# Linear attention feeding a swish MLP: the load of k of batch 5 issued one block sooner

## The chip, the cores and the metric

The kernel runs on one core of a Trainium2 chip. The metric is device time in microseconds (us) of one execution; the figure for a kernel is the median of its runs. The core has five engines that run beside each other and wait for each other through semaphores: TensorE (PE, matrix products), VectorE (DVE), ScalarE (ACT, activation functions), GpSimd (POOL) and SyncE (SP, which here only starts transfers). Transfers run on 16 DMA engines, fed from queues that an engine's instructions fill.

## The reference

Eight batches of 8 heads, 576 positions and head size 64. First a linear attention with phi(x) = elu(x) + 1, then a two-layer MLP with a swish of learned slope.

```
q_p, k_p = phi(q), phi(k)                 # phi(x) = where(x > 0, x, exp(x) - 1) + 1
kv  = einsum('bhsd,bhse->bhde', k_p, v)
z   = sum(k_p, axis=2)
num = einsum('bhsd,bhde->bhse', q_p, kv)
den = einsum('bhsd,bhd->bhs', q_p, z)[..., None] + 1e-06
x   = (num / den).transpose(0, 2, 1, 3).reshape(4608, 512)
h   = x @ w_in                            # 512 -> 2048
g   = h * (1.0 / (1.0 + exp(-beta * h)))
out = g @ w_out                           # 2048 -> 512
```

## The kernel before, in words

Work is cut by batch. The 576 positions of a batch become four tiles of 128 and a rest of 64; the rests of all eight batches are gathered in `xT_tail` and make a ninth block. A block b of the MLP has an `h_phase` (16 groups of four matmuls, each 128 x 512, into one bank of the four-bank pool `mmps`, each followed by a silu on ACT, lines 454 and 462) and a `y_phase` (four output tiles of 16 matmuls, line 472, evacuated by DVE at line 245 and stored). Batch 0 has a prologue of its own; the loop at line 842 runs the blocks 1 to 8.

The attention of later batches is threaded into these phases as side work. `at(sh, n, ...)` puts a call behind group n of the h phase, `at(sy, n, ...)` behind step n of the y phase (16 steps of four matmuls). In block b, with n = b + 1 and m = b + 2:

- the y phase computes phi of q of batch m (`phi_all(m, "q")`, step 3), starts its transposes by DMA (`q_trans_dma(m)`, tile `qTd`, step 5), and loads q of batch m + 1 (`load_q`, step 5) held by `hold` until the last of these transposes has landed;
- for b below 3, phi of k of batch m is computed there too (step 8);
- from b = 2 on, the two exps of k of batch m + 1 are put at step 10 (`phi_exps`), and the DVE part of phi comes at group 2 of the next h phase (`phi_rest`);
- x of batch n is transposed by DMA from SP (`x_trans_dma`, tiles `xT` and `xT_tail`), and v of batch m + 1 is loaded from SP (step 9).

The order on each engine is the order in which the program emits the calls (a manual schedule). ACT therefore runs the silus of block b + 1 behind the exps emitted in block b. Between exp and silu ACT loads a function table (1.28 us).

Loads of q and k go out from POOL's queue and convert to bf16 on the way. k lives in three buffers `xk`, batch b in `xk[b % 3]`, q likewise in `xq`, so k of batch 5 takes the buffer of batch 2. The exp results `e` have four buffers, two for each phi. Names that the trace shows: `xk<-in_k_dram` is a load of k (line 83), `e<-xk` an exp of k (line 144), `r<-xk` the DVE part (line 148), `g<-h_ps` a silu (line 462).

Before the change k of batch 4 is loaded in block 1, and in block 2 k of batch 5 and k of batch 6 are loaded one behind the other, both behind the held q of batch 5. From block 3 on k is loaded two batches ahead of the phi of q in the same block.

Of the kernel before, what the change touches and what calls it, by code (L numbers as in the profile page):

```python
# [16 lines left out]
def kernel(  # L17
# [62 lines left out]
    def load(eng, dst, src, b, h0=0, n=4):  # L80

        rows = src[b].rearrange("h (g j) d -> (h g) (j d)", j=J)
        return eng.dma_start(  # L83
            out=dst[:, h0 : h0 + n].rearrange("p h j d -> p h (j d)"),
            in_=rows.rearrange("(i p) e -> p i e", p=P)[:, h0 : h0 + n],
        )
# [140 lines left out]
    def num_tile(name):  # L227
        return numps.tile([P, 2, 512], F32, tag="num", name=name)
# [4 lines left out]
    def kv_both(b):  # L233

        t = num_tile("kvp")
        for pr in range(2):
            kv_pair(b, pr, [t[:, hh, pr * EA : (pr + 1) * EA] for hh in range(2)])
        st[b, "kvd"] = work.tile([P, 2, 2 * EA], BF16, tag="kv_bd", name="kvd")
        nc.vector.tensor_copy(st[b, "kvd"], t[:, :, 0 : 2 * EA])
# [32 lines left out]
    def q_trans_dma(b):  # L272
        st[b, "qTd"] = work.tile([P, 4 * J, G], BF16, tag="qT", name="qTd")
        for hh in range(2):
            st[b, "qTd", "dma"] = nc.sync.dma_start_transpose(
                out=st[b, "qTd"][:, hh * 2 * J : (hh + 1) * 2 * J],
                in_=st[b, "q"][hh * G : (hh + 1) * G].rearrange("p a j c -> p (a j c)"),
            )

    def q_odd_trans(b, tp):  # L280

        tv = tp.rearrange("p (a n) -> p a n", a=2)
        for pr in range(2):
            nc.tensor.matmul(
                tv[:, pr], st[b, "q"][:, pr, J - 1, :], identity,
                is_transpose=True, start=True, stop=True, skip_group_check=True,
            )
        nc.scalar.copy(
            q_odd[b].rearrange("p (i a) g -> p a i g", i=2),
            tv.rearrange("p a (i g) -> p a i g", i=2),  # L290
        )
# [30 lines left out]
    def numers(b, after=None):  # L322

        pairs = [num_tile("nps") for _ in range(2)]
        odd = [mm_tile("nps_m") for _ in range(2)]
        if after is not None:
            for pr in range(2):
                kv_pair(after, pr, [pairs[pr][:, hh, 6 * EA : 7 * EA] for hh in range(2)])
        for k in range(2):
            dst = [pairs[k][:, h] for h in range(2)]  # L330
            numer_tile(b, dst, k)
            numer_tile(b, dst, 2, (k,), 4)
        numer_tile(b, odd, 3)
        for hh in range(2):
            quads(b, odd, 4 + hh, lambda c: (c, J - 1), hh, None)
        st[b, "nps"] = pairs, odd
        for k in range(3):
            norms(b, k)
        if after is not None:
            st[after, "kvd"] = work.tile([P, 2, 2 * EA], BF16, tag="kv_bd", name="kvd")  # L340
            for pr in range(2):
                nc.vector.tensor_copy(
                    st[after, "kvd"][:, :, pr * EA : (pr + 1) * EA],
                    pairs[pr][:, :, 6 * EA : 7 * EA],
                )
# [93 lines left out]
    def x_trans_dma(b, t):  # L439
        xv = st[b, "xs", t].rearrange("p n d -> p (n d)")  # L440
        if t < NT - 1:
            nc.sync.dma_start_transpose(out=x_dst(b, t), in_=xv)
            return

        for pr in range(2):
            nc.sync.dma_start_transpose(  # L446
                out=xT_tail[:, places(b, pr), b * G : (b + 1) * G],
                in_=xv[pr * G : (pr + 1) * G, 0 : 2 * P],
            )
# [39 lines left out]
    def load_q(b, after):  # L489
        if b < B:  # L490
            hold(load(nc.gpsimd, xq[b % NX], q, b), after)

    def load_k(b):
        if b < B:
            load(nc.gpsimd, xk[b % NX], k, b)

    def load_v(b):
        if b < B:
            load(nc.sync, vf[b % 2], v, b)

    def phi_exps(b, a):
        for pr in range(2):
            phi_part(b, a, pr, xin(b, a, pr))

    def phi_rest(b, a):
        phi_tile(b, a)
        for pr in range(2):
            phi_relu(b, a, pr, xin(b, a, pr))
        for pr in range(2):
            phi_min(b, a, pr)  # L510

    def phi_all(b, a):
        phi_exps(b, a)
        phi_rest(b, a)

    def v_copies(b):
        for pr in range(2):
            v_copy(nc.gpsimd, b, pr)
# [288 lines left out]
    def h_phase(b, x, side):  # L807
        for ff in range(FC):

            if b == 1 and ff in (3, 4):  # L810
                hp = num_tile("h_ps2")[:, 0]
            else:
                hp = mm_tile("h_ps")
            h_mm(b, x, ff, hp)
            silu(b, ff, hp)
            run(side, ff)

    def y_phase(b, side, last=False):
        for t in range(4):
            if last and t == 3:  # L820
                for c0, c1 in ((0, 320), (320, 512)):
                    yp = mm_tile("y_ps")
                    for i in range(4):
                        y_mm(b, t, i, yp, c0, c1)
                    y_out(b, t, yp, c0, c1, (nc.sync, nc.scalar))
                break
            yp = mm_tile("y_ps")
            halves = ((0, 256), (256, 512)) if b == 1 and t > 1 else ((0, 512),)
            for cols in halves:
                for i in range(4):  # L830
                    y_mm(b, t, i, yp, *cols)
                    if i < 3 and cols is halves[-1]:
                        run(side, 4 * t + i)
            y_out(b, t, yp)
            run(side, 4 * t + 3)

    def at(side, n, *fs):
        side.setdefault(n, []).extend(fs)
# [3 lines left out]
    for b in range(1, B + 1):  # L842
        n = b + 1
        m = n + 1
        sh, sy = {}, {}
        if b == 1:
            at(sh, 0, lambda: q_trans_dma(2))
            at(sh, 1, lambda: v_copies(2))
            at(sh, 2, lambda: load_q(3, st[2, "qTd", "dma"]), lambda: load_k(3))
            at(sh, 2, lambda: load_v(3))  # L850
            at(sh, 7, lambda: q_odd_trans(1, num_tile("qop")[:, 0].bitcast(BF16)[:, 0:256]))
            at(sh, 8, lambda: kv_both(2))
            at(sy, 1, lambda: numers(2))
        elif n < B:
            if b == 2:
                at(sh, 8, odd_numers, odd_norms, lambda: kv_both(3))
                at(sh, 9, lambda: [x_trans_dma(i, 4) for i in range(2)])
            if b == 3:
                at(sh, 8, lambda: kv_both(4))
            if 4 < m < B:  # L860
                at(sh, 2, lambda: phi_rest(m, "k"))
                at(sh, 6, lambda: v_copies(m))
            at(sh, FC - 1, lambda: numers(n, m if 4 < m < B else None))
        if n < B:
            for t in range(NT):
                at(sy, t // 3 + (2 if b == 1 else 0), lambda t=t: x_trans_dma(n, t))
        if m < B:
            at(sy, 3, lambda: phi_all(m, "q"))
            at(sy, 5, lambda: q_trans_dma(m), lambda: load_q(m + 1, st[m, "qTd", "dma"]))
            if b < 3:  # L870
                at(sy, 5, lambda: load_k(m + 1))
                at(sy, 4, lambda: v_copies(m))
                at(sy, 8, lambda: phi_all(m, "k"))
            if b > 1:
                at(sy, 5, lambda: load_k(m + 2))
            at(sy, 9, lambda: load_v(m + 1))
            if 4 < m + 1 < B:
                at(sy, 10, lambda: phi_exps(m + 1, "k"))
        h_phase(b, xT[b % 3] if b < B else xT_tail, sh)
        y_phase(b, sy, last=(b == B))  # L880
# [30 lines left out]
```

## Time and profile before

| | |
|---|---|
| median of 3 runs | 303.47 us (302.96 to 306.81) |
| span of the profiled run | 302.5 us |
| PE busy | 277.7 us, 92% |
| ACT busy | 160.3 us, 53% |
| DVE busy | 108.0 us, 36% |
| POOL busy | 36.8 us, 12% |
| loads of k, full batches | 7 of 576 KB each, median 13.8 us from issue to landing |
| loads of q | 7 of 576 KB each, median 9.6 us |
| mean granted TensorE clock | 0.972 |

Busy time of an engine is the sum of its instructions' spans. Where a view gives a duration and, in brackets, a time with an arrow, the bracket is how long the engine was idle just before and what released it. A wait that the trace puts down to one engine may have had several semaphores; the one that came last is named. The row of slices shows the span in 40 equal parts, each digit the busy share in tenths; the row of the clock shows in the same way what share of full speed the array was granted.

### The profile page before, as it was taken

Reading aid. Unit: us, or ns where it says so; the run is one execution under the profiler, and the core shown is the slowest. Engines: PE = TensorE matmul, PEld = TensorE weight load, DVE = VectorE, ACT = ScalarE, POOL = GpSimd, SP = SyncE. Lnnn points to the kernel's source line nnn. Section 1 sums busy time; section 2 is a strip of 40 time slices with the busy share of each in tenths; the row PEclk is TensorE's granted clock in tenths of the full one; section 3 lists DMA queues with packets and bytes.
Section 4 is the critical chain, followed back from the end, with each engine's and each line's share of the span. In section 5 each row is a group of like instructions: output and inputs, shape, how many; then the busy total and the mean of one; then the engine's idle time right before and its main releaser. Section 6 shows DMA issues by size and latency. Waiting matters only on the chain.

```text
span 302.5 us, 5979 instructions
## 1 busy us (share of the span) xinstructions
PE 277.7 (92%) x2482; PEld 139.7 (46%) x2512; DVE 108.0 (36%) x259; ACT 160.3 (53%) x219; POOL 36.8 (12%) x51
## 2 busy tenths in 40 slices
PE   7899999999999960199999999999999999999995
PEld 2674466447544420045444544454444444444443
DVE  5824489439114810301931274046106100120012
ACT  5888569939467300658718852791372057108600
POOL 8622002140040022000003100300000000000000
PEclk9999999999999996579999999999999999999999
DMA  8999999499499389700379737913801430131022
GB/s 220 206 246 361 275 211 233 85 262 165 111 273 156 78 198 274 121 2 2 74 132 266 139 77 161 280 34 64 200 15 38 107 77 0 35 69 37 0 68 72
DMA packets 51723, 41.03 MB, mean 136 GB/s; under 512 B 31584, under 2 KB 43120, under 8 KB 51696
## 3 DMA queue, kind: packets, MB, share of 16 engines
q1 hardware_dynamic: 38800, 23.61, 32.7%
q0 software_dynamic: 12736, 16.91, 28.7%
q8 instruction: 19, 0.31, 0.4%
q10 hardware_dynamic: 160, 0.13, 0.2%
q14 instruction: 8, 0.07, 0.1%
HBM read 36.71 MB, written 9.44 MB: 153 GB/s over the span
## 4 chain that ended last, share of the span: by engine, by line
PE 81%; DMA 9%; DVE 4%; ACT 2%; SPq 2%; issue 2%; POOL 0%; DVEq 0%; POOLq 0%; ACTq 0%
PE h_ps L454 38%; PE y_ps L472 37%; DMA xk<-in_k_dram 4%; DMA xT_tail<-xs 3%; SPq L446 1%; DMA qTd<-phi_q 1%; DMA stage<-in_q_dram 1%; ACT e L144 1%; PE h_ps L665 1%; PE nps L184 1%; DVE phi_q L155 1%; PE kvp L184 1%; DVE r L148 1%; PE nps L309 1%; DVE y_sb L245 1%
## 5 line engine op out<-in xcount | busy, mean ns | idle before, releaser
L462 ACT ACTIVATE g<-h_ps,beta_c 128x512 bf16<-128x512 f32 x144 | 97.5, 689 | 84.8 <-PE h_ps L454 84.3
L472 PE MATMUL y_ps<-w_out,g 128*128 128x512 bf16 (+4 forms) x621 | 126.5, 359 | 0.9 <-issue 0.2
L454 PE MATMUL h_ps<-xT,w_in 128*128 128x512 bf16 x486 | 111.3, 385 | 17.4 <-ACT g L462 16.8
L454 PEld LDWEIGHTS <-w_in 128*128 128x128 bf16 x560 | 55.0, 99 | 83.7 <-issue 20.6
L472 PEld LDWEIGHTS <-g 128*128 128x128 bf16 x636 | 60.9, 98 | 61.1 <-DVE xs_odd L383 0.3
L245 DVE COPY y_sb<-y_ps 128x512 f32<-128x512 f32 (+2 forms) x37 | 24.9, 672 | 77.4 <-PE y_ps L472 77.4
L144 ACT ACTIVATE e<-xk 128x1152 bf16<-128x1152 bf16 x16 | 17.8, 1154 | 23.8 <-DMA xk<-in_k_dram 23.7
L392 DVE TENSOR_SCALAR den<-nps 128x12 f32<-128x12 f32 x12 | 2.0, 165 | 57.4 <-PE nps L309 57.4
L83 POOL DMA_DIRECT2D xq<-in_q_dram x7 | 5.2, 745 | 107.6 <-DMA qTd<-phi_q 89.5
L144 ACT ACTIVATE e<-xq 128x1152 bf16<-128x1152 bf16 x14 | 15.6, 1155 | 0.8 <-DMA xq<-in_q_dram 0.8
L454 PE MATMUL h_ps<-xT_tail,w_in 128*128 128x512 bf16 x62 | 13.9, 379 | 0.1
L155 DVE TENSOR_TENSOR phi_q<-e,r 128x1152 bf16<-128x1152 bf16 (+2 forms) x17 | 12.5, 765 | 2.7 <-ACT e L144 2.4
L173 POOL CAST vaug<-vf 128x1152 bf16<-128x1152 f32 x10 | 11.2, 1151 | 17.9 <-DMA vf<-in_v_dram 13.3
L383 DVE TENSOR_TENSOR xs<-nps,rden 128x512 bf16<-128x512 f32 (+1 forms) x24 | 12.3, 552 | 1.0 <-DMA xT_tail<-xs 0.4
L144 ACT ACT_TABLE_LOAD x6 | 7.7, 1283 | 8.5 <-DMA xq<-in_q_dram 8.4
L148 DVE TENSOR_SCALAR r<-xk 128x1152 bf16<-128x1152 bf16 x16 | 6.7, 457 | 15.2 <-DMA xk<-in_k_dram 15.2
L155 DVE TENSOR_TENSOR phi_k<-e,r 128x1152 bf16<-128x1152 bf16 x16 | 11.6, 750 | 0.6 <-ACT e L144 0.6
L133 PE MATMUL warm_ps<-xT 128*128 128x512 bf16 x20 | 7.5, 532 | 1.8 <-DVE xT L96 1.5
L462 ACT ACT_TABLE_LOAD x6 | 7.7, 1283 | 0.1
L83 POOL DMA_DIRECT2D xk<-in_k_dram x9 | 6.8, 753 | 4.5 <-DMA g<-in_moe_w_out_dram 2.0
L148 DVE TENSOR_SCALAR r<-xq 128x1152 bf16<-128x1152 bf16 x14 | 6.8, 517 | 1.0 <-DMA xq<-in_q_dram 1.0
L730 DVE TENSOR_SCALAR w_out<-g,rbeta 128x512 bf16<-128x512 f32 x8 | 3.8, 536 | 9.0 <-DMA g<-in_moe_w_out_dram 9.0
(98 smaller groups left out, 117.8 us busy)
## 6 DMA issues: line engine op xcount, KB each, us to landing
out_dram<-y_sb SPq DMA_DIRECT2D x70, 128.0 KB, 2.5
vf<-in_v_dram SPq DMA_DIRECT2D x5, 1152.0 KB, 6.6
xq<-in_q_dram POOLq DMA_DIRECT2D x7, 576.0 KB, 9.6
xk<-in_k_dram POOLq DMA_DIRECT2D x7, 576.0 KB, 13.8
w_in<-in_moe_w_in_dram POOLq DMA_DIRECT2D x4, 512.0 KB, 12.8
g<-in_moe_w_out_dram POOLq DMA_DIRECT2D x2, 1024.0 KB, 17.7
stage<-in_moe_w_out_dram POOLq DMA_DIRECT2D x2, 1024.0 KB, 20.8
stage<-in_q_dram SPq DMA_DIRECT2D x2, 576.0 KB, 4.0
```

What stands on the lines that cost most here:

```text
L83: return eng.dma_start(out=dst[:, h0 : h0 + n].rearrange("p h j d -> p h (j d)"), in_=rows.rearrange("(i p) e -> p i e", p=P)[:, h0 : h0 + n],
L133: nc.tensor.matmul(warm_ps[:, 0:cols], warm[:, 0:P], warm[:, 0:cols], start=True, stop=True)
L144: nc.scalar.activation(st[b, a, pr, "e"][:, :, j0:j1], x[:, :, j0:j1], ACTF.Exp)
L148: nc.vector.tensor_scalar(r, x, 0.0, 1.0, ALU.max, ALU.add)
L155: nc.vector.tensor_tensor(st[b, a][:, pr, j0:j1].rearrange("p j (h d) -> p j h d", h=2), st[b, a, pr, "e"][:, :, j0:j1].rearrange("p h j d ...
L173: eng.tensor_copy(vaug[b % 2][:, pr, :, :, 0:D], src[:, places(b, pr)].rearrange("p h j d -> p j h d"))
L184: nc.tensor.matmul(dst[hh][c], st[b, "k"][r, pr, j, c], mov(r, j, h), start=(j == 0), stop=(j == J - 1), skip_group_check=True,)
L245: eng.tensor_copy(dst, src)
L383: nc.vector.tensor_mul(out, num, rd[..., None].to_broadcast(list(num.shape)))
L454: nc.tensor.matmul(hp[:, c0:c1], w_in_sb[ff // 4][:, kc, (ff % 4) * P : (ff % 4 + 1) * P], x[:, kc, c0:c1], start=(kc == 0), stop=(kc == K ...
L462: nc.scalar.activation(g_sb[b % 2][:, ff, :], hp, ACTF.Silu, scale=beta_c[:, ff : ff + 1])
L472: nc.tensor.matmul(yp[:, c0:c1], g_sb[b % 2][:, ff, t * P : (t + 1) * P], w_out_sb[i][:, c, c0:c1], start=(ff == 0), stop=(ff == FC - 1), ...
```

## The change

The load of k of batch 5 is moved from block 2 to block 1. In block 1, `load_k(4)` is now followed by `load_k(5)` at the same step of the y phase; in block 2, behind the held q of batch 5, only `load_k(6)` is left. Later blocks keep their loads. It is meant to have k of batch 5 in its buffer without waiting for q of batch 5, which is held by the transposes of batch 4.

```
             at(sy, 5, lambda: q_trans_dma(m), lambda: load_q(m + 1, st[m, "qTd", "dma"]))
             if b < 3:
-                at(sy, 5, lambda: load_k(m + 1))
                 at(sy, 4, lambda: v_copies(m))
                 at(sy, 8, lambda: phi_all(m, "k"))
-            if b > 1:
-                at(sy, 5, lambda: load_k(m + 2))
+            if b == 1:
+                at(sy, 5, lambda: load_k(m + 1))
+            at(sy, 5, lambda: load_k(m + 2))
             at(sy, 9, lambda: load_v(m + 1))
```

## The prediction

> **What bounds the kernel now.** I started with the slices of the page. Each slice is 302.5 / 40 = 7.56 us.
>
> ```profile
> PE   7899999999999960199999999999999999999995
> ACT  5888569939467300658718852791372057108600
> PEclk9999999999999996579999999999999999999999
> ```
>
> TensorE (PE) is busy in nine tenths or more of nearly every slice, so it sets the time. There is one hole, in slices 14 to 16 counted from 0 (106 to 128 us), with ScalarE (ACT) empty just before the end of it, and the granted clock falls to 6, 5 and 7 tenths in and after it. The groups then say who waited for whom.
>
> ```profile
> L462 ACT ACTIVATE g<-h_ps,beta_c 128x512 bf16<-128x512 f32 x144 | 97.5, 689 | 84.8 <-PE h_ps L454 84.3
> L454 PE MATMUL h_ps<-xT,w_in 128*128 128x512 bf16 x486 | 111.3, 385 | 17.4 <-ACT g L462 16.8
> L144 ACT ACTIVATE e<-xk 128x1152 bf16<-128x1152 bf16 x16 | 17.8, 1154 | 23.8 <-DMA xk<-in_k_dram 23.7
> ```
>
> The first line is ACT waiting for PE, harmless. The second is the reverse: the h matmuls of line 454 waited 16.8 us for a silu. The third gives the reason: the exps of k waited 23.7 us for a load of k. The chain of waits, taken for 104 to 130 us, puts them in order (start, length, what):
>
> ```profile
> 106.72 3.76 DMA qTd<-phi_q
> ...
> 111.04 0.46 POOL xq L83
> ...
> 111.78 11.65 DMA xk<-in_k_dram
> ...
> 123.51 2.22 ACT e L144 x2
> 125.75 1.28 ACT L462
> 127.04 0.69 ACT g L462
> ```
>
> So at b = 2 the transpose of phi(q) of batch 4 lands, GpSimd (POOL) may then issue q of batch 5 and behind it k of batch 5, that k lands at 123.4, ACT does its two exps and a table load, and only then the first silu of block 3. The timeline of ACT shows which batch each exp belongs to, since it follows program order:
>
> ```profile
> 99.04 2.22 ACT L144 ACTIVATE e<-xk 128x1152 bf16<-128x1152 bf16 x2 [0.63 <-DMA xk<-in_k_dram]
> 123.51 2.22 ACT L144 ACTIVATE e<-xk 128x1152 bf16<-128x1152 bf16 x2 [22.26 <-DMA xk<-in_k_dram]
> ```
>
> The first pair is k of batch 4 (step 8 of y_phase(2)), the second k of batch 5 (step 10). PE had started block 3 at 107.39, filled the four banks of mmps with 16 matmuls by 111.01, and stood until 127.78.
>
> **What the Trainium skill says.** "TensorE: Matmul & The Clock Gate", Part 1, says that an idle array falls to half clock and regains it after about 3.4 us of work. The trace agrees in kind: clock 0.50 in 127.78 to 131.00, 0.75 in 131.00 to 134.77, 1.00 after. The same page (on the architectural detail of the array) says ACT's queue is strict FIFO; the trace agrees, silus whose matmuls had ended by 111 ran at 127.04. "DMA: Bandwidth & Descriptors", section on queues, rings and completion order, says that each DMA engine takes one ring in order and alternates between rings by packets. The trace fits: q and k of batch 4 were issued on GpSimd's queue 0.73 us apart and landed at 94.8 and 99.0, one after the other, while transposes on SyncE's queue beside them took 5 to 9 us instead of 2.4.
>
> **The change, part by part.**
>
> Removed: k of batch 5 from the queue at 111.8, behind q of batch 5. Added: the same 576 KB load at b = 1, right behind q and k of batch 4. Those were issued at 83.63 and 84.36, so k of batch 5 goes out at about 85.1. Nothing holds it there: xk has three buffers and batch 5 takes that of batch 2, whose last reader was done by about 50 us. POOL gets 0.75 us more of issue work at 85.1; it is then idle until 89.09 waiting for v, so that costs nothing. At b = 2 it gets 0.75 us less. No instruction is added or dropped in sum.
>
> When does it land? Behind k of batch 4, which landed at 84.36 + 14.6 = 98.98. Steps from a q to the k behind it, from issue times and landings: 3.6 us (67.9 to 71.5), 4.1 (94.8 to 99.0), 2.8 (120.6 to 123.4), 3.0 (169.2 to 172.2). So 101.6 to 103.1; I take 102.5. ACT is done with the exps of batch 4 at 101.26, and the next e buffer is free after the two phi_q of batch 4 at 102.57 and 103.25. The exps end at about 104.7, the table load of 1.28 us at 106.0. The first h group of block 3 ends near 108.25, so ACT is ready 2 us before it is wanted. PE would only stand if the first silu ended after 111.01, which by 2.22 + 1.28 + 0.73 means a landing after 106.8: 3.7 us of slack against the latest of the four steps.
>
> What it gives is the length of block 3 set against its neighbours, from the list of the chain's pieces and the windows:
>
> ```profile
> 107.39:111.01 3.62, 3.62 (x17) 1.55 (x16) 0.69 (x1) 0.00 (x0) 0.00 (x0) 1.00 0.80 192
> 111.01:127.78 16.77, 0.00 (x1) 0.00 (x0) 2.35 (x4) 4.24 (x5) 4.47 (x5) 0.64 0.97 209
> 127.78:131.00 3.22, 3.22 (x8) 1.17 (x8) 0.00 (x0) 2.37 (x4) 0.00 (x0) 0.50 0.00 0
> 131.00:134.77 3.77, 3.77 (x21) 1.39 (x23) 0.00 (x0) 2.06 (x3) 0.00 (x0) 0.75 0.00 0
> ```
>
> (Columns: window, length, then busy of PE, weight load, DVE, ACT, POOL, then clock.) Block 3 ran from 107.39 to 156.96, 49.57 us. Block 4, 156.96 to 186.02, took 29.06. Block 3 does the same plus one group of 72 small kv matmuls at its step 8 (0.73). So undisturbed it takes 29.8, and **the gain is 49.57 - 29.8 = 19.75**. Made up from its parts: the stand 16.77, and the cold restart, where 20 matmuls took 6.99 us against 20 x 0.216 = 4.32 at the rate of block 4 (37 in 7.99), so 2.67; together 19.44. The two agree within 0.3. I take 19.7.
>
> What is moved costs: packets of k of batch 5 now run from 99 to about 103 beside SyncE's transposes. The one that matters is the last xT of batch 3, issued 100.21, landed 102.5, wanted by PE at 107.39. Bounds: nothing, or 5.1 us as xT took at 94.4 (lands 105.3, no cost), or 9.3 as the slowest xT_tail (lands 109.5, 2.1 us). I take nothing. The transposes of phi(q) of batch 4 go out at 105.33, after it. The y stores hold nobody.
>
> Does a later wait take its place? With block 3 whole, PE wants things 19.7 us sooner. v of batch 5 is issued at 109.78 as before and copied by 118.8; its kv products would be wanted at 141.6 - 19.7 = 121.9: 3.1 us of slack, and less traffic beside it. q of batch 5 (landed 120.6) would be wanted by ACT at 124.0. k of batch 6 moves up into the place of k of batch 5 (123.4) and is wanted at 126.1; even late, ACT has no silu due there until block 4. Blocks 4 and later run as before, shifted: in block 4 k of batch 7 came 172.2 for 174.9 and nobody waited.
>
> Sum: 303.47 - 19.7 = **283.8 us**.
>
> **Rivals.**
>
> A, a part of the hole stays because k of batch 5 lands late. For it: the queues are full from 83 to 99 (summed DMA share 1.2). Against: 3.7 us of slack, and share 0.36 in 99 to 103, where it will run. A landing at 109 gives 2.2 us of stand: 286.0.
>
> B, its packets delay transposes or q and k of batch 4. For it: xT_tail transposes took up to 9.3 us there. Against: in-order rings leave everything before 99 as it was. Gives the 2.1 us above: 285.9.
>
> C, the early load is hidden behind a wait that was there anyway, and nothing is won. It would need something else to keep ACT until 123.5, and its waits name nothing but loads of q and k. 303.
>
> D, slower: the transposes pile up. If each of the four xT of batch 3 took 8.4 instead of 2.4, one after the other, the last lands at 102.5 + 24 = 126.5; PE stands 19.1 us and restarts cold for 2.7: 303.5 - 19.7 + 21.8 = 305.6, more if the qTd transposes then hold q. Against: one load of 576 KB adds about 4 us of traffic.
>
> **How the numbers follow.** Forecast 0.86, A 0.04, B 0.06, C 0.02, D 0.02. The range takes in A and B and half a microsecond of spread below with a somewhat better packed block 3: 282.6 to 286.5. Faster by over 2% (under 297.4): 0.96. Within 2%: C and most of D, 0.03. Slower: 0.01.
>
> **What would show it right or wrong.** Right: an xk load third in POOL's row near 85.1 and only one behind q near 111.8; the wait of the exps for xk of some 23.7 us down to under 3; the 16.8 us of h_ps behind the silu gone; PE's slices all 9 after the first and no dip of the clock; block 3 of about 29.8 us; everything later shifted by the same amount. Wrong at step one if k of batch 5 lands after 106.8; wrong at the transposes if PE starts block 3 later than 107.4; wrong at the later waits if a new stand appears near 122 (v of batch 5) or if blocks 4 to 7 take other than about 29 us.

## The result and the profile after

The changed kernel takes **285.25 us** (median of 4 runs, 285.16 to 285.57) against 303.38 us before (4 runs, 302.96 to 306.81). The ratio is 0.939 with a 95% interval of 0.9327 to 0.9453: 18.1 us less. The profiled execution has a span of 283.5 us. One run of a later experiment (e10: 291.72 us, mean granted clock 0.988 against 1.00 in its other runs, no trace) lies more than 1.5% above the fastest of its kernel and is left out of e10's median and ratio.

The slices of the page after, to be read against those of before:

```profile
PE   7899999999999999999999999999999999999994
PEclk9999999999999999999999999999999999999999
```

The hole in slices 14 to 16 is gone, and so is the dip of the clock behind it. PE is busy for 97% of the span (92% before). In the groups of the page the two waits that carried the argument have shrunk:

```profile
L454 PE MATMUL h_ps<-xT,w_in 128*128 128x512 bf16 x486 | 108.6, 379 | 0.6
...
L144 ACT ACTIVATE e<-xk 128x1152 bf16<-128x1152 bf16 x16 | 17.8, 1151 | 2.5 <-DVE y_sb L245 1.6
```

The h matmuls waited 17.4 us, now 0.6; the exps of k waited 23.8 us, now 2.5. The timeline of POOL after (start, length, what, idle before it) shows the move itself:

```profile
83.87 0.75 POOL L83 DMA_DIRECT2D xq<-in_q_dram  x1 [15.30 <-ACT g L462]
84.61 1.49 POOL L83 DMA_DIRECT2D xk<-in_k_dram  x2
...
110.75 0.75 POOL L83 DMA_DIRECT2D xq<-in_q_dram  x1 [19.09 <-ACT g L462]
111.49 0.76 POOL L83 DMA_DIRECT2D xk<-in_k_dram  x1
```

Two loads of k now follow q of batch 4, and only one is left behind q of batch 5. In the timeline of ACT the exps of batch 5 come 3.8 us after those of batch 4, no longer 24.5:

```profile
98.20 2.20 ACT L144 ACTIVATE e<-xk 128x1152 bf16<-128x1152 bf16 x2
102.04 2.22 ACT L144 ACTIVATE e<-xk 128x1152 bf16<-128x1152 bf16 x2 [1.64 <-DVE y_sb L245]
104.28 1.28 ACT L462 ACT_TABLE_LOAD   x1
```

One caution for the reader. The 1.64 us are put down to a copy of DVE, whose result these exps don't read. The load landed at 102.0: the two loads of k issued from 84.61 on took 13.4 us and, from their median of 15.0, 16.6 us. So that landing released the exps; the copy only ended at the same moment. In a second profile of the changed kernel (e5, below) the same wait is put down to the load:

```profile
100.62 2.22 ACT L144 ACTIVATE e<-xk 128x1152 bf16<-128x1152 bf16 x2 [1.04 <-DMA xk<-in_k_dram]
```

The length of block 3, from its first h matmul to that of block 4, is read in the windows. First before (block 3, block 4), then after (columns: window, length, busy of PE, weight load, DVE, ACT, POOL, clock, share of the DMA engines, GB/s):

```profile
107.39:156.79 49.40, 32.47 (x342) 14.98 (x344) 12.09 (x30) 21.06 (x25) 4.47 (x5) 0.83 0.53 109
156.79:185.86 29.07, 28.91 (x271) 13.73 (x272) 11.39 (x29) 17.89 (x22) 3.73 (x4) 1.00 0.70 161
```

```profile
107.82:137.77 29.95, 29.79 (x342) 14.39 (x344) 11.82 (x30) 17.88 (x22) 3.74 (x4) 1.00 0.73 156
137.77:166.84 29.07, 28.91 (x270) 13.72 (x272) 11.40 (x29) 17.88 (x22) 3.73 (x4) 1.00 0.70 162
```

Block 3 became 19.45 us shorter with the same 342 matmuls, and block 4 has the same length to the hundredth. Block 3 itself starts 0.43 us later (107.82 for 107.39). So the whole gain lies in block 3. That leaves a question: the profiles show 19.45 us, the medians 18.1.

### The profile page after: what moved, and what is told of

Read it like the earlier page. It is cut to its first block, busy times and chain, and to the rows that moved or that the text cites. A ratio compares the mean times of both kernels' runs of the same rounds, so it can differ in the third digit from the quotient of the medians.

```text
span 283.5 us, 5980 instructions
## 1 busy us (share of the span) xinstructions
PE 275.2 (97%) x2482; PEld 139.3 (49%) x2512; DVE 107.9 (38%) x259; ACT 160.5 (57%) x219; POOL 37.8 (13%) x51
## 4 chain that ended last, share of the span: by engine, by line
PE 94%; DMA 2%; DVE 1%; issue 1%; ACT 1%; POOLq 0%
PE y_ps L472 44%; PE h_ps L454 43%; DMA xk<-in_k_dram 2%; PE h_ps L665 1%; PE nps L184 1%; PE nps L309 1%; PE kvp L184 1%; DVE phi_k L155 1%; PE nps_m L309 0%; ACT e L144 0%; PE nps L631 0%; PE tp L655 0%; PE nps L563 0%; PE nps L265 0%; PE dps L546 0%
## 5 line engine op out<-in xcount | busy, mean ns | idle before, releaser
L454 PE MATMUL h_ps<-xT,w_in 128*128 128x512 bf16 x486 | 108.6, 379 | 0.6
L454 PEld LDWEIGHTS <-w_in 128*128 128x128 bf16 x560 | 54.4, 98 | 64.8 <-DVE xT L437 0.3
L184 PEld LDWEIGHTS <-phi_k 64*64 64x64 bf16 x576 | 5.6, 106 | 3.1 <-issue 2.1
## 6 DMA issues: line engine op xcount, KB each, us to landing
xk<-in_k_dram POOLq DMA_DIRECT2D x7, 576.0 KB, 13.4
w_in<-in_moe_w_in_dram POOLq DMA_DIRECT2D x4, 512.0 KB, 12.2
```

The source lines that it names most:

```text
L184: nc.tensor.matmul(dst[hh][c], st[b, "k"][r, pr, j, c], mov(r, j, h), start=(j == 0), stop=(j == J - 1), skip_group_check=True,)
L454: nc.tensor.matmul(hp[:, c0:c1], w_in_sb[ff // 4][:, kc, (ff % 4) * P : (ff % 4 + 1) * P], x[:, kc, c0:c1], start=(kc == 0), stop=(kc == K ...
```

## The experiments

Two things were open: where the missing 1.3 us are, and which wait comes next. "Stand" is PE's wait inside or ahead of block 3. The first theory (K) is that of the prediction: only the landing of k of batch 5 counts, against a limit set by ACT's queue. The rival is B of the prediction: the packets of an early load delay the transposes of x, and PE starts block 3 late.

**How constant is the hole? (e1, e12)** The kernel before, unchanged, profiled twice more.

> The kernel before once more, for its profile. Open is why the gain in the medians (18.1 us) is smaller than the 19.45 us by which block 3 became shorter in the profiles. Theory: the profiled execution of before (304.28 us) was one with a long wait; here the total is near 303.4 and the stand of PE in block 3 is shorter than 16.77 us, by up to 0.9. Rival: the stand is the same within 0.1 and the start of the kernel (up to block 3) differs by some tenths of a us from run to run.

> The kernel before a third time, for its profile: the stand of PE in block 3 was 16.77 us and then 15.69, with 6.99 and 6.31 us for the 20 matmuls behind it. Theory: its total follows these two terms, between 302 and 304.3 us. Rival: another part of the kernel varies as much.

PE's timeline in block 3, of the second execution and then of the third:

```profile
126.50 6.31 PE L454 MATMUL h_ps<-xT,w_in 128*128 128x512 bf16 x20 [15.69 <-ACT g L462]
```

```profile
127.38 6.80 PE L454 MATMUL h_ps<-xT,w_in 128*128 128x512 bf16 x20 [16.37 <-ACT g L462]
```

| execution of before | time | stand | 20 matmuls after it | block 3 |
|---|---|---|---|---|
| first | 304.28 us | 16.77 | 6.99 | 49.40 |
| second | 302.33 us | 15.69 | 6.31 | 47.64 |
| third | 303.69 us | 16.37 | 6.80 | 48.82 |

Stand and restart of the second execution are 1.76 us below the first, of the third 0.59; the times are 1.95 and 0.59 below. So in these three executions nearly all of the scatter comes out of the hole, and the execution I took for the prediction was a long one. The rivals fall: no other part varied as much, and the start of block 3 moved by 0.19 us at most (107.20 for 107.39). My size for e1 was too small, though: the stand fell by 1.08 us, not by up to 0.9, and the total came 1.1 us below the 303.4 I had expected.

**What is the slow restart? (e2)** Matmuls that nobody reads are put where PE stands, in the kernel before.

```
             h_mm(b, x, ff, hp)
+            if b == 3 and ff == 3:
+                fill = num_tile("fill")[:, 0]
+                for _ in range(72):
+                    nc.tensor.matmul(
+                        fill, w_in_sb[0][:, 0, 0:P], w_in_sb[0][:, 0, :], start=True, stop=True
+                    )
             silu(b, ff, hp)
```

> The kernel before with 72 matmuls more in block 3, put on PE where it stands waiting (72 x 0.216 = 15.6 us of the 16.77). Their result is read by nobody. Theory: the wait for k of batch 5 stays as it is, but the array stays warm, so the 20 matmuls behind it take 4.3 us and not 6.99: 2.7 us less than before, 300.7 us, clock 1.00 all through. Rival: the slow restart has another cause (the silus that come in a burst, PSUM banks): no gain, 303.4 us.

301.34 us (5 runs), ratio to before 0.9929 (0.9903 to 0.9956), so 1.3 to 2.9 us less. PE's timeline:

```profile
111.20 15.70 PE L818 MATMUL fill<-w_in 128*128 128x512 bf16 x72
127.39 4.48 PE L454 MATMUL h_ps<-xT,w_in 128*128 128x512 bf16 x20 [0.49 <-ACT g L462]
```

The wait for the load is as long as ever (the exps of batch 5 start at 123.12), yet the same 20 matmuls take 4.48 us, and the granted clock is 1.00 all through the run. The clock is what made them slow; its part is 6.70 - 4.48 = 2.2 us over the mean of the three executions above, not the 2.67 that I took from the first with a full-clock time of 4.32.

**A whole block sooner, or only out of the line? (e3)** k of batch 5 stays in block 2 and is put ahead of the held q.

```
             at(sy, 3, lambda: phi_all(m, "q"))
+            if b == 2:
+                at(sy, 5, lambda: load_k(m + 1))
             at(sy, 5, lambda: q_trans_dma(m), lambda: load_q(m + 1, st[m, "qTd", "dma"]))
+            if b == 1:
+                at(sy, 5, lambda: load_k(m + 1))
             if b < 3:
-                at(sy, 5, lambda: load_k(m + 1))
```

> k of batch 5 stays in block 2 but is issued ahead of the held q of batch 5. Theory (only the place behind the held q counts): POOL comes to it right after its copies of v, at about 91.5 us, it lands near 102, 285.3 us, as with the change. Rival (it must go out a whole block sooner, since the queues of block 2 are full): it lands after 107 and PE stands for some us, 288 to 295 us.

285.37 us (4 runs, ratio 0.9412, 0.9379 to 0.9446). POOL issued it at 90.37, it took 10.0 us, and the exps ran at 101.00; the last thing they waited for was now a buffer that DVE read from. ACT's timeline, then PE's:

```profile
101.00 2.22 ACT L144 ACTIVATE e<-xk 128x1152 bf16<-128x1152 bf16 x2 [1.42 <-DVE phi_q L155]
107.72 7.93 PE L454 MATMUL h_ps<-xT,w_in 128*128 128x512 bf16 x36
```

The 36 matmuls run without a stand, and the time is that of the changed kernel: what counted was the place behind the hold, not the block.

**Without the hold (e4)** The order of before, but q of batch 5 isn't held.

```
-            hold(load(nc.gpsimd, xq[b % NX], q, b), after)
+            d = load(nc.gpsimd, xq[b % NX], q, b)
+            hold(d, after) if b != 5 else None
```

> Order of the loads as before, but q of batch 5 is no longer held by the transposes of phi(q) of batch 4; q of batch 5, k of batch 5 and k of batch 6 all go out at about 91.5 to 93 us. Theory: k of batch 5 is third in line behind k of batch 4, lands near 105, below the limit of about 107: 285.3 us, at most 286. Rival (the hold protects the transposes of batch 3 and 4, which share the DMA engines): the last xT of batch 3 or the qTd of batch 4 land late and PE stands at the start or the end of block 3: 287 us or more.

287.13 us (4 runs, 0.9457, 0.9422 to 0.9492): the rival's number. k of batch 5 landed where I had expected it, and it wasn't what PE waited for. ACT's timeline, then PE's, of this run:

```profile
105.05 2.22 ACT L144 ACTIVATE e<-xk 128x1152 bf16<-128x1152 bf16 x2 [4.96 <-DMA xk<-in_k_dram]
```

```profile
109.78 7.93 PE L454 MATMUL h_ps<-xT,w_in 128*128 128x512 bf16 x36 [2.13 <-DMA xT<-xs]
```

Block 3 began 2.13 us late, because the last transpose of x of batch 3, issued at 99.27, took 10.4 us. The hold that made k of batch 5 late also protects these transposes, so my theory was incomplete.

**How much room is left? (e5 to e8)** The changed kernel again, and with one, two and three loads in front of k of batch 5, into memory that nobody reads (`pad`, three parts of `stage`).

```
+            if b == 1:
+                at(sy, 5, lambda: [load(nc.gpsimd, pad[i], k, 4) for i in range(1)])
             at(sy, 5, lambda: load_k(m + 2))
```

(As in e6; `range(2)` in e7, `range(3)` in e8. The line that defines `pad` is left out here.)

> The changed kernel once more, as the base for the three runs beside it. 285.3 us; block 3 29.95 us; k of batch 5 landing near 102 us. Theory: the total differs from the first profile only in the first 20 us. Rival: block 3 itself varies by some tenths of a us.

> The changed kernel with one load more of 576 KB (k of batch 4 into a buffer that nobody reads) between k of batch 4 and k of batch 5. Theory: k of batch 5 lands some 3 to 4 us later, near 105.5; the limit, from when PE fills its four banks (111.4) less exps, table load and one silu (4.23), is 107.2; no stand, 285.3 us. Rival (packets beside the transposes of batch 3 cost): last xT lands later than 107.8 and PE starts block 3 late, 286 to 288 us.

> The changed kernel with two such loads in front of k of batch 5. Theory: landing near 109, 1.8 us over the limit of 107.2; PE stands about 1.8 us and stays warm: 287 us. Rival as above: in addition a late start of block 3, 288 to 290 us.

> The changed kernel with three such loads. Theory: landing near 112.5, PE stands about 5.3 us, and a part of the cold restart comes with it (0 to 2.7): 290.5 to 293 us. Rival: the landing of k of batch 5 isn't what PE waits for; the time grows by less than half of the growth of the landing.

| | median | k of batch 5 landed | last xT issued, took, landed | PE starts block 3 |
|---|---|---|---|---|
| e5, none | 284.79 us (284.77 to 284.97) | 100.5 | 98.47 + 3.9 = 102.4 | 107.38 |
| e6, one | 284.74 us (284.63 to 285.35) | 104.6 | 99.01 + 7.1 = 106.1 | 107.22 |
| e7, two | 287.29 us (286.42 to 289.28) | 107.8 | 99.18 + 9.7 = 108.9 | 108.99 |
| e8, three | 292.0 us (290.4 to 292.41) | 112.7 | 99.74 + 13.3 = 113.0 | 113.18 |

Block 3 is as long in e5 as in the first profile, and the 0.44 us between the two are there at the first h matmul already (19.48 and 19.92 us), as I had expected of e5. The totals of e7 and e8 are near those I had written down, but for the wrong reason. PE's timeline of e7 and of e8:

```profile
108.99 7.93 PE L454 MATMUL h_ps<-xT,w_in 128*128 128x512 bf16 x36 [1.64 <-DMA xT<-xs]
```

```profile
113.18 9.62 PE L454 MATMUL h_ps<-xT,w_in 128*128 128x512 bf16 x36 [5.10 <-DMA xT<-xs]
```

PE waits at the first matmul of the block and for a transpose, not after 16 matmuls for a silu. But in these runs both landings move together, so they don't separate the two causes.

**Full queues, k of batch 5 early (e9)** The three loads go behind k of batch 5 instead of in front of it.

```
             at(sy, 5, lambda: load_k(m + 2))
+            if b == 1:
+                at(sy, 5, lambda: [load(nc.gpsimd, pad[i], k, 4) for i in range(3)])
```

> The changed kernel with three loads of 576 KB that nobody reads, now BEHIND k of batch 5, so that k of batch 5 lands near 102 us as with the change, while the queues stay as full as in the run with three loads in front. Theory X (the last transpose of x of batch 3 doesn't land before the loads on GpSimd's queue have run dry, and this sets the start of block 3): last xT lands near 113 us, PE stands some 5 us at the start of block 3, 290.5 to 292.5 us. Theory K (it was the landing of k of batch 5 that counted in those runs): 284.8 to 285.4 us.

292.61 us (4 runs, 0.9651, 0.9611 to 0.9691), as with the loads in front. The exps of batch 5 ran at 100.48 and ACT was free at 104.0, yet PE's timeline says:

```profile
111.47 10.77 PE L454 MATMUL h_ps<-xT,w_in 128*128 128x512 bf16 x36 [4.10 <-DMA xT<-xs]
```

The last of the loads landed at 110.7, and the last xT took 12.2 us (99.12 to 111.3). This shows the rival's mechanism by itself. 36 matmuls took 10.77 us where e5 needs 7.93, so the stand of 4.10 us cost 2.84 more through the clock. The windows of e9 and of e8 show PE at half clock behind the stand (the 0.50 in each line):

```profile
111.47:117.25 5.78, 5.78 (x14) 2.02 (x15) 2.76 (x5) 1.84 (x3) 1.50 (x2) 0.50 1.00 219
```

```profile
113.28:116.70 3.42, 3.42 (x9) 1.22 (x8) 2.61 (x5) 3.39 (x4) 0.00 (x0) 0.50 0.99 223
```

**k of batch 5 late, transposes undisturbed (e10, e11)** As e3, but held by a transpose of batch 3: the last xT (t = 3), or the last of the rest (t = 4).

```
-            nc.sync.dma_start_transpose(out=x_dst(b, t), in_=xv)
+            st[b, "xd", t] = nc.sync.dma_start_transpose(out=x_dst(b, t), in_=xv)
...
             at(sy, 3, lambda: phi_all(m, "q"))
+            if b == 2:
+                at(sy, 5, lambda: hold(load(nc.gpsimd, xk[2], k, 5), st[3, "xd", 3]))
             at(sy, 5, lambda: q_trans_dma(m), lambda: load_q(m + 1, st[m, "qTd", "dma"]))
+            if b == 1:
+                at(sy, 5, lambda: load_k(m + 1))
             if b < 3:
-                at(sy, 5, lambda: load_k(m + 1))
```

(As in e10; `st[3, "xd", 4]` in e11. The same mark is set at the transposes of the rest, left out here.)

> k of batch 5 in block 2, ahead of q of batch 5, but held until the last xT of batch 3 has landed: late, and with no packet beside the transposes of x. It is issued near 103 us and lands near 109 (6.0 us was the shortest time of such a load). Theory K (limit for its landing 107.2 us, counted from when PE has filled its four banks): PE starts block 3 on time, stands for a silu after 16 matmuls, some 1.8 us, and stays warm: about 287 us. Theory X alone: no stand, 285 us.

> As the run before, held until the last transpose of the rest of batch 3 has landed, some 2.5 us later: issued near 105.5, landing near 111.5. Theory K: PE stands some 4.3 us after 16 matmuls, with 0 to 2.7 us of a cold restart: 289 to 292 us, about 2.5 us or more over the run before. Theory X alone: 285 us.

287.70 us (3 runs, 0.9483, 0.9444 to 0.9523) and 294.96 us (4 runs, 0.9721, 0.9687 to 0.9755), the second over the 289 to 292 that I had expected. PE's timeline of e10, then of e11:

```profile
107.45 2.75 PE L454 MATMUL h_ps<-xT,w_in 128*128 128x512 bf16 x12
110.73 1.02 PE L454 MATMUL h_ps<-xT,w_in 128*128 128x512 bf16 x4 [0.53 <-DVE y_sb L245]
113.43 4.48 PE L454 MATMUL h_ps<-xT,w_in 128*128 128x512 bf16 x20 [1.67 <-ACT g L462]
```

```profile
107.49 3.62 PE L454 MATMUL h_ps<-xT,w_in 128*128 128x512 bf16 x16
118.99 6.09 PE L454 MATMUL h_ps<-xT,w_in 128*128 128x512 bf16 x20 [7.88 <-ACT g L462]
```

Here PE starts on time and stands after 16 matmuls, for a silu (in e10 it also waits 0.53 us for a copy of DVE ahead of the last four). In e10 the load was issued at 102.01 and took 7.1 us, in e11 at 105.25 and 9.4 us: landings at 109.1 and 114.6. Both loads took longer than I had assumed, which is why e11 missed its number; transposes of phi(q) ran beside them, in e11 also the load of v of batch 5 (issued at 110.16), but no run separates these causes. The restart follows 4.3 us behind the landing in both, and in the kernel before too (123.43 and 127.78). Theory K's limit is real. After 1.67 us of standing the 20 matmuls ran at full clock (4.48 us), after 7.88 us at half clock to begin with (6.09 us).

So there are two limits for the start of block 3, each shown by itself. k of batch 5 must land by about 106.7 (the banks are full near 111.0, less 4.3), and the loads on POOL's queue must have run dry early enough for the last xT to land by 107.4. The second is the nearer one once more bytes go ahead of it. The changed kernel keeps both. None of the kernels tried beats it by more than the runs differ.

## Why the prediction was right, and where its number was off

Direction, mechanism and place were right: 285.25 us measured, 283.8 forecast, range 282.6 to 286.5.

- **Issue and landing.** Forecast about 85.1 and 102.5; measured 85.3 and 102.0, and 100.5 in e5. (The low end of the forecast, 101.6, is a slip: 98.98 + 2.8 is 101.8.)
- **ACT free.** Forecast 106.0; measured 104.28 + 1.28 = 105.56.
- **The extra issue on POOL costs nothing.** Held: the copies of v start at 89.42 (89.09 before), still waiting for v.
- **Later waits.** v of batch 5 was copied by 118.64, its kv products came at 122.56; q of batch 5 landed at 120.5, its exps ran at 124.67. No stand, and block 4 takes 29.07 us.
- **What is moved costs.** I took nothing, with a bound of 5.1 us for the last xT. It took 3.9 us (2.3 before), landed at 103.8 and cost nothing. But I set the slack by the landing of k of batch 5 alone, 3.7 us. e6 to e9 show that the transposes have the nearer limit: one load more leaves 1.1 us (106.1 for 107.22), two cost 2.5 us in time.
- **Rivals.** A didn't come about in the changed kernel; e10 and e11 show what it costs when it does. B was given too little room. Its reason to fail, that rings in order leave everything before 99 us as it was, held for the loads of q and k of batch 4, but not for the transposes: the first xT of batch 3 was issued at 94.89 and landed at 102.4, where before it went from 94.42 to 99.5. Nothing came of it because, as the prediction had counted, some 4 us were left between the landing of the last xT (103.8) and PE's start of block 3 (107.8). C and D didn't occur.
- **The term that was mis-sized** is the gain of 19.7 us, which is 1.6 above the 18.1 of the medians. (1) About 0.25: I ended block 3 in one view and began it in another, and took the extra kv group at 0.73 where it adds 29.95 - 29.07 = 0.88; the same profiles give 19.45. (2) About 0.9: I took the hole from one execution, 304.28 us long, off a median of 303.4; e1 and e12 show that its length varies with the hole. The mean block 3 of the three executions is 48.62, which gives 18.7. (3) About 0.4: the first profile after starts block 3 at 107.82 instead of 107.39. Its chain begins with the first load of k (landed at 7.76 us), that of before with the first load of q. In e5 block 3 starts at 107.38, so I take this for scatter between executions. These few profiles don't prove it: the medians of the runs made along with e5 differ by 18.0 us all the same (302.83 and 284.79).

What the Trainium skill says of the array's clock ("TensorE: Matmul & The Clock Gate", Part 1) carried a term of the sum, and e2 confirms the cause with 4.48 against 6.31 to 6.99 us. The time to full clock was not the 3.4 us of the prediction, though: the clock came back 5.11, 3.75 and 4.74 us after the restart in the three executions of before.

That each DMA engine alternates between rings by packets ("DMA: Bandwidth & Descriptors", on queues, rings and completion order) I had taken for the reason why transposes beside loads took 5 to 9 us. The traces agree with it in kind: in e8 the four xT of batch 3 landed at 103.73, 107.47, 112.55 and 113.04, and the loads beside them at 101.58, 105.14, 108.83 and 112.71, so both went on together. What I had missed is the sum of it: PE needs the last of the four.

## What to carry to other kernels

When an engine's in-order queue has work for a later stage ahead of work for the next one, a late load for the later stage stops everything behind it: look for which load the queue stands at, and what that load itself stands behind. A hold that protects one transfer delays everything issued behind it on the same queue, so put what needs no protection ahead of it, but count who shares the DMA engines in that stretch before you send more there. And when a gain is the removal of a wait, measure that wait in several executions; here it was the part of the kernel that varied most.

## What the hardware showed that I had not expected

- A DMA transpose of 128 x 512 that takes 2.3 us with free queues took 3.9, 7.1, 9.7 and 13.3 us in e5 to e8, with none, one, two and three loads of 576 KB more on another queue, issued 12 to 15 us earlier. It landed 0.3 to 1.9 us after the last of these loads each time (112.7 and 113.0 with three, 102.0 and 103.8 in the first profile after). This doesn't mean that a transpose waits until the other queue has run dry. The one in question is the last of four; in e8 the four were issued at 94.93, 96.33, 97.61 and 99.74, and the first three landed at 103.73, 107.47 and 112.55, all ahead of the last load. While loads were queued there, about one of these transposes landed for each load, 3.7 to 5.1 us apart, and the last followed 0.3 us behind the last load. Three others are ahead of the last xT on its queue and landed late too; that they hold it is inferred, not tested.
- The slow restart is no fixed price, and the length of the stand doesn't set it: 20 matmuls took 6.99, 6.31, 6.80 and 6.09 us after stands of 16.77, 15.69, 16.37 and 7.88 us, and 4.48 after 1.67. A stand of 4.10 us cost 2.84 us more over the next 36 matmuls, one of 5.10 us only 9.62 - 7.93 = 1.69. What sets it is how long PE then works at half clock: 5.78 us in e9 and 3.42 in e8, as the windows above show, 3.31 in e11, and 5.11, 3.75 and 4.74 in the three executions of before. The price is about half of that in each (2.84, 1.69, 1.61, 2.51, 1.83 and 2.32 us). In the traces the clock stays at half for 3.41 us (e8), 6.83 (e9 and e11) or 17.07 us (the three of before), which are one, two and five times 3.41; the price depends on how much of such a stretch is left when PE starts again. After stands of 1.64, 1.67 and 2.13 us (e7, e10, e4) the clock hadn't fallen at all.
